# First batch of a two-stage kernel: row and channel DFT as plain matmuls on TensorE in place of VectorE folds, with the sine tables ahead of the first exponential

## The chip, the cores and the metric

The kernel runs on one core of a Trainium2 chip. The metric is the device time of one execution in microseconds (us); lower is better. All times below are of that one core. The engines are called as in the profile: PE (TensorE, matmuls), DVE (VectorE), ACT (ScalarE), POOL (GpSimd), SP (the queue that issues most transfers).

## What is computed

There are 8 batches of 8 heads, with 576 rows and 64 values to a head. First comes an attention with feature maps, then a Fourier mixing of the whole 576 x 512 block of a batch, a normalisation and a two-layer network (FFN):

```python
proj = einsum('bhsd,df->bhsf', x, w_phi); proj -= max(abs(proj), -1)
phi = concatenate([exp(proj), exp(-proj)])
num = einsum('bhsf,bhfd->bhsd', phi(q), einsum('bhsf,bhsd->bhfd', phi(k), v))
x = num / (einsum('bhsf,bhf->bhs', phi(q), sum(phi(k))) + 1e-6)   # (8, 576, 512) over heads
u = x + real(fft(fft(x, axis=1), axis=2))
un = (u - mean(u)) / sqrt(var(u) + 1e-6)
out = u + relu(un @ w_ch1) @ w_ch2                                # 512 -> 2048 -> 512
```

## The kernel before

The work of a batch b is split into streams, Python generators that issue a few instructions for each step: keys, queries and values are fetched (K, Q, V), turned (A, B; for batch 0 on PE: G, J), projected and exponentiated (P, T, R, S), combined and mixed (M, with D for the folds), normalised (N, U) and sent through the FFN (F). One-off streams are C (arguments of the sines), H (the sine tables), Z (constant pads), W (the FFN's weights) and Y (fill matmuls of ones, result unused, in `stir`). A string `PLAN` of one letter a step says in which order the steps are issued; each engine runs its instructions in that order, and waits where an operand isn't there. So the order of an engine's queue is fixed by PLAN, and the times are not.

The FFN of batch 0 can begin when its input `UT` is there; until then PE has only the attention of batches 0 and 1, the mixing of batch 0 and the fill. From then on the FFN of one batch runs beside the attention and mixing of the next.

The mixing of a batch is a real DFT over 576 rows and then over 512 channels. The 576 rows of X lie in 5 chunks of 128 partitions (the last half full). `folded` uses the symmetry of sines and cosines: DVE adds and subtracts mirrored rows and mirrored channels of X into R (lines 869 to 893), subtracts a term of row 0 that a matmul with ones has spread over the partitions (pm, lines 994, 998 and 1048) and folds once more into CEO (line 1007, 1053). PE then needs only 3 chunks: `along_rows` multiplies with the tables CS and SS (cosine and sine over rows, psD and px, lines 1019 to 1058), ACT and DVE copy psD to DT and ET, and the channel DFT multiplies with CD and SD (pu, line 1087). DVE adds pu to X (line 1072 for batch 0), UN is X less its mean, four transposes on PE turn it (put, line 1142) and DVE or ACT copies it to UT (lines 1146, 1148). The first FFN matmul (psf, line 1207) needs chunks 0 and 2 of UT.

For batch 0, the tables SS, CS, SD, CD are made by four ACT sines (lines 212 to 223), behind the last exponential of batch 0. ACT has to load a function table when it changes between exponentials and sines. The arguments are made by DVE and POOL (`constants`, lines 175 to 204). At the start, ACT loads the exponentials' table and runs `warm`.

In PSUM, `pb` has three buffers for psD, pu, put, psq and psf, `pj` two for psk and psh, and `pk` one. A matmul waits until the buffer that it takes has been read. KT is batch 1's turned keys (transfers of line 387 on SP, from KS, which POOL's line 258 fetches); psk is their projection (line 468), MK its largest absolute values (line 488).

Of the kernel before, what the change touches and what calls it, by code (L numbers as in the profile page):

```python
# [9 lines left out]
AT = mybir.ActivationFunctionType  # L10
# [13 lines left out]
    "CYCCZYCYGGTRTTGZZGTYZWRTJTSRJGRJYSTPTSPKTTPJMJRTSSKMYMBMPTQPTPQVTMZTMQTMMTPCMMMTTMTHDYAMMYHHDHHKYYVD"  # L24
    "YDTMTMHTKZMRMSRTYMTTMNYMRVTYQNNMTNTSMNMBFFFRFFNUFNFSMFWFUNRUFQUMTPSFFMNTFPSMTFTNUPYFQMUFPPTVMFTPMTPF"
    "FMMFTTFMFAUTFMMFFMFMFMFMFFKRFPDFFTTTFFDVFFDRFTFFVDFFKTSRFQVFFFFMFFMTFRFFFFFSMTMFFMRTFFMSTMFTFNNMFMQF"
    "PTMMFTFSFMPTFFPTTPMFFFFMFSNBFMFPTQMFFAFMNPFTFMNMFFMFFMMFTTFFURMFFVFRMFFSTFFMFFMFVFTTPFFFFRFPDFFFTPFF"
    "FFFVDDRFFFQFDTMTFFQTSMKFFFMFFFKMRMFTTTMMFNNFFMMFMQFMFFSSMTFMTFFFNFSTPPMFTFMBFPTFPAMFFFMFNTFKMMFFFNFM"
    "FMFFMFFUMQMFFVMFFFTTPFFFFMTFFRFTTFFVFFFRFFRFDFFFFDFDFFDPTFMFTTFFFFMKFRFTMSFMRFFMFTSPMFNTMPQNSFFFFQMM"
    "MMTTTFFBMSFFFFTPMTFSFFMFFMTPVMFFFFMTPNFFNNMMMFFMAFFFMUFMFKMFFFMFFTTDTTFRFFSFFFFRVFFTMFFFFFRPTFFDFFFD"  # L30
    "RFFFTDFMFVKTPFFFFFMTMBQMFFRSFMFTSTSTMMKFFFNNSFMMFMMFTFMFPTMKFFFFPTPMTFFMFFFNMFTPPMFFFTNFQMNMVFFMFQMF"
    "MFFMUFFMFFVMAFFFFTTTTFDRFRFFTFSFFFFMRFFQFFFDFFTFFFDFFRFVDFTFMFFTTMFFMFFMFRSMFQTTTMFTQFNFMSVFFMFFTNPM"
    "MFMSTPMTFFFFSMTPPMFTFFMPPFBAFMFPFMFNNFMMVFMFMFFFMTTFRMNUFFFFFMRFFFMFFFSTFFMFFPTFFTFFFDDFFFRFTFFFDFDV"
    "RFFFMFTTFFMFMTMFRFFSMFFSFMTTNTFFMFNMMFFFMMFTFMPSTFNFFFPTFMFFTMPFFFFMPSPMFFTMFFPFTMNFFFNMFMFFFUMFMFMF"
    "FFFMFFMFMFFFFFDFFDFFFFFDFFFDFMFFFMFMFFMMFFMFNFMNFFFFFFMFFFFFMNFFFMFFNFFFFFFFFFFFFFFFNUFFFFFFFFFFFFFF"
    "FFFFFFFFFFFFFFFFFFFFFFFFFFFFFFFFFFFFF"
# [4 lines left out]
def kernel(  # L41
# [81 lines left out]
    nc.vector.memset(mhalf[:], -0.5)  # L123
    keep = const.tile([128, 1], F32, name="keep")
# [18 lines left out]
    def count_first():  # L143
# [12 lines left out]
        nc.vector.tensor_single_scalar(out=ident[:], in_=tn, scalar=0.0, op=ALU.is_equal)  # L156
# [3 lines left out]
    def count_rest():  # L160
        count(pick_i[:], [[1, 32]], 0, -1)
        nc.vector.tensor_single_scalar(
            out=pick_i[:], in_=pick_i[:], scalar=31, op=ALU.bitwise_and
        )
        nc.vector.tensor_scalar(
            out=pick[:], in0=pick_i[:], scalar1=0.0, scalar2=-2.0, op0=ALU.is_equal, op1=ALU.mult
        )
        nc.vector.tensor_copy(out=ident_b[:], in_=ident[:])
# [3 lines left out]
    turns, turns_c = gs[:, 1024:1024 + 3 * NK], gc[:, C:2 * C]  # L172

    def constants(b):
        nc.vector.tensor_scalar_mul(out=pn[:, 0:3], in0=pc[:, 0:3], scalar1=1.0 / S)
        nc.vector.tensor_scalar_mul(out=pn[:, 3:4], in0=pc[:, 3:4], scalar1=1.0 / C)
        for j in range(3):
# [3 lines left out]
            nc.gpsimd.tensor_scalar(  # L181
                out=turns[:, NK * j:NK * j + NK], in0=rs, scalar1=pn[:, j:j + 1], scalar2=MAGIC,
                op0=ALU.mult, op1=ALU.add,
            )
        yield
# [23 lines left out]
    def sines(b):  # L209
# [20 lines left out]
        yield  # L230

# [8 lines left out]
    def pads(b):  # L240
        for X_ in (QPHP, QPHN):
            nc.gpsimd.memset(X_[:, :, 576:640], 1.0)
            yield
        for X_ in (V4P, V4N):
# [54 lines left out]
    def load_first():  # L299
# [17 lines left out]
        nc.scalar.activation(out=warm[:], in_=halfpi[:], func=AT.Exp)  # L317
# [580 lines left out]

    def first_heads():
        X = xpool.tile([128, 5, C + 1], F32, tag="X", name="X")  # L900
        R = fpool.tile([128, 3, 2, 512], F32, tag="R", name="R")
        CEO = fpool.tile([128, 3, 2, 2, 128], BF16, tag="CEO", name="CEO")
        HI = HIS[0]
        folds[0] = folded(X, R, HI)

# [31 lines left out]
        return X, R, CEO, HI  # L937

    def heads(b):
        if b == 0:  # L940
            return (yield from first_heads())
# [49 lines left out]
    def mixing(b):  # L991
        X, R, CEO, HI = yield from heads(b)
# [21 lines left out]
        def along_rows(i, mat, dst):  # L1014
            if b == 0:
                for mt in range(2):
                    ps = pb.tile([128, 512], F32, tag="pb", name="psD")
                    for c in range(3):
                        nc.tensor.matmul(
                            ps[:, 0:NF], lhsT=CEO[0:deep[c], c, abs(mt - i), i, :],  # L1020
# [370 lines left out]
```

## Time and profile before

| | |
|---|---|
| median of 3 runs | 414.81 us (414.77 to 420.89) |
| profiled execution, its own time | 415.15 us |
| its span, first to last instruction | 413.4 us |
| mean granted PE clock | 0.995 |
| busy: PE, DVE, ACT, POOL | 394.6, 319.4, 303.8, 215.1 us |
| PE busy in us 0 to 50 and 50 to 100 | 43.2 and 47.8 us |
| last value of batch 0's X (line 919) ready | 34.9 us |
| first FFN matmul (line 1207) starts | 50.90 us |
| first matmul of the FFN of batch 1 starts | 104.45 us |

The profile covers one execution. A row of the timeline has the start in us, the length in us, the engine, the line, the instruction with the tiles that it writes and reads, and in brackets the idle time ahead of it with what ended that. PE's rows overlap, because matmuls are pipelined: two rows of the same form with different counts give the time of one more matmul. A row of the windows has, for each engine, its busy time in that stretch and the number of instructions, then the granted PE clock.

### The profile page before, as it was taken

Reading aid. Unit: us, or ns where it says so; the run is one execution under the profiler, and the core shown is the slowest. Engines: PE = TensorE matmul, PEld = TensorE weight load, DVE = VectorE, ACT = ScalarE, POOL = GpSimd, SP = SyncE. Lnnn points to the kernel's source line nnn. Section 1 sums busy time; section 2 is a strip of 40 time slices with the busy share of each in tenths; the row PEclk is TensorE's granted clock in tenths of the full one; section 3 lists DMA queues with packets and bytes.
Section 4 is the critical chain, followed back from the end, with each engine's and each line's share of the span. In section 5 each row is a group of like instructions: output and inputs, shape, how many; then the busy total and the mean of one; then the engine's idle time right before and its main releaser. Section 6 shows DMA issues by size and latency. Waiting matters only on the chain.

```text
span 413.4 us, 10526 instructions
## 1 busy us (share of the span) xinstructions
PE 394.6 (95%) x4194; PEld 259.5 (63%) x4194; DVE 319.4 (77%) x662; ACT 303.8 (73%) x617; POOL 215.1 (52%) x279
## 2 busy tenths in 40 slices
PE   7898999989999989999899999999999999999994
PEld 3574577535856568566756577566856586658563
DVE  5979887999699867797689878888799768875101
ACT  6988999658958886688868886789758885544350
POOL 8997695774466753707658373649271343201000
PEclk9999899999999999999999999999999999999999
DMA  7999979898674899654965979757952141106103
GB/s 210 221 170 158 181 100 185 87 118 128 102 118 58 67 179 141 63 92 83 129 97 65 156 104 142 80 72 116 117 97 52 46 83 21 27 14 114 24 23 90
DMA packets 108520, 42.71 MB, mean 103 GB/s; under 512 B 82615, under 2 KB 103479, under 8 KB 108471
## 3 DMA queue, kind: packets, MB, share of 16 engines
q0 software_dynamic: 46272, 16.60, 37.1%
q1 hardware_dynamic: 61703, 24.85, 32.9%
q10 hardware_dynamic: 496, 0.59, 0.6%
q8 instruction: 33, 0.54, 0.5%
q14 instruction: 16, 0.13, 0.1%
HBM read 36.77 MB, written 9.44 MB: 112 GB/s over the span
## 4 chain that ended last, share of the span: by engine, by line
PE 69%; DVE 13%; DMA 8%; ACT 4%; POOL 3%; issue 2%; DVEq 0%; POOLq 0%; SPq 0%; ACTq 0%
PE psf L1207 29%; PE pso L1224 19%; DMA UT<-UN 4%; PE kv L853 3%; PE psD L1035 2%; PE psk L468 2%; DMA KT<-KS 2%; PE pu L1087 2%; DMA KS<-in_k_dram 2%; PE psq L522 2%; PE psh L563 1%; DVE MK L488 1%; PE pso L1250 1%; DVE cb L969 1%; DVE X L1077 1%
## 5 line engine op out<-in xcount | busy, mean ns | idle before, releaser
L1207 PE MATMUL psf<-UT,W1b 128*128 128x320 bf16 (+1 forms) x1024 | 141.1, 286 | 2.9 <-DMA UT<-UN 2.8
L1224 PE MATMUL pso<-W2b,HT 128*128 128x512 bf16 x496 | 120.5, 379 | 0.0
L1207 PEld LDWEIGHTS <-W1b 128*128 128x128 bf16 x1024 | 94.6, 98 | 30.9 <-issue 3.8
L1212 ACT ACTIVATE HT<-psf 128x320 bf16<-128x320 f32 x128 | 53.9, 444 | 25.7 <-PE psf L1207 19.5
L1224 PEld LDWEIGHTS <-HT 128*128 128x128 bf16 x496 | 45.2, 98 | 43.2 <-issue 0.4
L975 POOL TENSOR_TENSOR X<-cb,rd 128x640 f32<-128x640 f32 x28 | 35.1, 1254 | 52.9 <-DVE rd L973 29.6
L443 POOL TENSOR_TENSOR VCn<-VS,VCn 128x512 bf16<-128x512 bf16 x28 | 29.9, 1067 | 43.4 <-ACT VCn L438 36.6
L530 DVE TENSOR_REDUCE MQ<-psq 128x8 f32<-128x1024 f32 (+1 forms) x32 | 34.3, 1088 | 17.8 <-PE psq L522 17.4
L1230 DVE SCALAR_TENSOR_TENSOR X<-pso,rs,X 128x512 f32<-128x512 f32 x31 | 23.0, 743 | 28.2 <-PE pso L1224 28.0
L1214 ACT ACTIVATE HT<-psf 128x512 bf16<-128x512 f32 x64 | 37.3, 602 | 6.8 <-PE psf L1207 6.6
L488 DVE TENSOR_REDUCE MK<-psk 128x8 f32<-128x1024 f32 x28 | 33.8, 1210 | 1.4 <-ACT KPn L474 1.4
L474 ACT ACTIVATE KPp<-psk 128x1024 bf16<-128x1024 f32 x28 | 28.8, 1027 | 7.8 <-PE psk L468 7.5
L258 POOL DMA_DIRECT2D QS<-in_q_dram x49 | 33.4, 688 | 1.1 <-issue 1.1
L1133 ACT ACTIVATE UN<-X,MV 128x512 bf16<-128x512 f32 (+1 forms) x35 | 25.2, 726 | 11.5 <-DVE MV L1158 8.0
L572 ACT ACTIVATE QPHP<-psh 128x1024 bf16<-128x1024 f32 x28 | 28.9, 1031 | 4.8 <-PE psh L563 4.5
L474 ACT ACTIVATE KPn<-psk 128x1024 bf16<-128x1024 f32 x28 | 28.7, 1025 | 1.7 <-DVE MK L488 1.6
L443 POOL TENSOR_TENSOR VCp<-VS,VCp 128x512 bf16<-128x512 bf16 x28 | 29.9, 1067 | 0.0
L572 ACT ACTIVATE QPHN<-psh 128x1024 bf16<-128x1024 f32 x28 | 29.0, 1036 | 0.0
L1157 DVE BATCH_NORM_STATS2 st<-X 128x6 f32<-128x512 f32 (+1 forms) x40 | 27.1, 678 | 0.2
L1077 DVE TENSOR_TENSOR X<-pu,X 128x512 f32<-128x512 f32 (+3 forms) x49 | 23.5, 526 | 4.6 <-PE pu L1087 4.5
L955 PEld LDWEIGHTS <-QPHP 128*128 128x128 bf16 x280 | 20.5, 99 | 7.8 <-DVE cb L969 3.8
L1173 POOL TENSOR_TENSOR rs<-VE,mhalf 128x5 f32<-128x5 f32 (+1 forms) x9 | 10.3, 1148 | 24.8 <-DVE VE L1172 24.7
(462 smaller groups left out, 797.2 us busy)
## 6 DMA issues: line engine op xcount, KB each, us to landing
out_dram<-X SPq DMA_DIRECT2D x31, 128.0 KB
out_dram<-X SPq DMA_DIRECT2D x15, 256.0 KB
KS<-in_k_dram POOLq DMA_DIRECT2D x7, 512.0 KB, 8.2
VS<-in_v_dram POOLq DMA_DIRECT2D x14, 256.0 KB, 4.8
W1b<-in_moe_w_ch_dram POOLq DMA_DIRECT2D x1, 2048.0 KB, 15.3
W2b<-in_moe_w_ch_dram POOLq DMA_DIRECT2D x1, 2048.0 KB, 16.1
QS<-in_q_dram POOLq DMA_DIRECT2D x28, 64.0 KB, 3.6
QS<-in_q_dram POOLq DMA_DIRECT2D x7, 256.0 KB, 5.6
```

Of the source, the lines that this page charges most:

```text
L258: nc.gpsimd.dma_start(out=pieces[i][0], in_=pieces[i][1])
L443: nc.gpsimd.tensor_tensor(out=VC[:, hs, :, 0:D], in0=values[b][0][:, hs, :].rearrange("p h (j d) -> p h j d", d=D), in1=VC[:, hs, :, D:D + ...
L474: nc.scalar.activation(out=KP[:, hs, :, :].rearrange("p e (jp jj) f -> p jj (e jp) f", jj=2), in_=psk[:], func=AT.Exp, scale=sgn,)
L488: nc.vector.tensor_reduce(out=MK[:, 2 * pr:2 * pr + 2, :].rearrange("p e (jp jj) -> p jj (e jp)", jj=2), in_=tiles[pr][:], axis=AX.X, op=A ...
L530: nc.vector.tensor_reduce(out=o, in_=i[:], axis=AX.X, op=ALU.max, apply_absolute_value=True)
L572: nc.scalar.activation(out=o, in_=psh[:], func=AT.Exp, scale=sgn)
L975: nc.gpsimd.tensor_tensor(out=X[:, :, at:at + 2 * D].rearrange("p c (e d) -> p e c d", e=2), in0=cb[:, :, :, 0:D], in1=rd[:].to_broadcast( ...
L1077: nc.vector.tensor_tensor(out=to, in0=more, in1=to, op=ALU.add)
L1207: nc.tensor.matmul(ps, lhsT=W1b[:, cc, 128 * hh:128 * hh + 128], rhs=UT[:, cc, lo:hi], start=(cc == 0), stop=(cc == NCC - 1),)
L1212: nc.scalar.activation(out=HT[:, hh, lo:hi], in_=ps, func=AT.Relu, scale=-1.0)
L1214: nc.scalar.activation(out=HT[:, hh - 1:hh + 1, lo:hi], in_=psw[:].rearrange("p (a n) -> p a n", a=2), func=AT.Relu, scale=-1.0,)
L1224: nc.tensor.matmul(po[:], lhsT=HT[:, hh, at:at + 128], rhs=W2b[:, hh, :], start=(hh == 0), stop=(hh == NHH - 1),)
```

## The change

Batch 0 gets no folds. `less_first` only subtracts the spread row 0 from X and writes bf16 (XB); it works first on the outer quarters of channels (heads 0, 1, 6, 7), then on the inner ones. `first_rows` multiplies all 5 chunks of rows with the tables, 4 quarters by cosine and sine, 8 groups of 5 matmuls of 320 columns in place of 15 of 289, and copies each group (4 on DVE, 4 on ACT) to EO. `first_channels` sums 16 matmuls of 256 columns to one pu, three times, in place of 4. It needs further tables (`full`, and SN = -SS) that POOL and DVE derive from the four of the sines. XB, EO and the rest lie in R's and the tables' old space. Batches 1 to 7 keep the folds; their code only moves to `folded_rows`.

The sines come ahead of the first exponential: the first table that ACT loads is that of the sines, and it loads that of the exponentials once. DVE instead of POOL makes the first product of the sines' arguments (`turns`), and `ident`, `pick` behind it. `stir` has 7 steps instead of 15. PLAN is new in its first 500 letters or so, which are batches 0 and 1; the rest is the same.

```diff
-        nc.vector.tensor_single_scalar(out=ident[:], in_=tn, ...)   # in count_first
...
+        nc.vector.tensor_single_scalar(out=ident[:], in_=tn, ...)   # in count_rest
...
-            nc.gpsimd.tensor_scalar(
+            nc.vector.tensor_scalar(
                 out=turns[:, NK * j:NK * j + NK], in0=rs, scalar1=pn[:, j:j + 1], scalar2=MAGIC,
...
+        yield
+        count_rest()
...
+        for z, T_ in ((0, CD), (1, SD)):
+            nc.gpsimd.tensor_tensor(
+                out=full[:, z], in0=T_[:].rearrange("p (k m) -> p k m", k=2),
+                in1=flip[:].unsqueeze(1).to_broadcast([128, 2, 256]), op=ALU.mult,
+            )
...
+        nc.vector.tensor_single_scalar(out=SN, in_=SS[:], scalar=-1.0, op=ALU.mult)
...
-        nc.scalar.activation(out=warm[:], in_=halfpi[:], func=AT.Exp)
+        nc.scalar.activation(out=warm[:], in_=halfpi[:], func=AT.Sin)
...
+    def less_first(X, XB, PM):
+        HI = HIS[0][:].rearrange("p i (a n) -> p (i a) n", n=128)
...
+        for outer in (True, False):
+            qs = slice(0, 4, 3) if outer else slice(1, 3)
+            nc.scalar.copy(out=HI[0:1, qs], in_=XQ[0:1, 4, qs])
+            pm = pb.tile([128, 2, 128], F32, tag="pb", name="pm")
+            nc.tensor.matmul(pm[:], lhsT=ones_b[:], rhs=HI[:, qs], start=True, stop=True)
+            if outer:
+                nc.scalar.copy(out=PM, in_=pm[:])
+            yield
+            for cs in (slice(0, 2), slice(2, 4)):
+                late = outer and cs.start
+                (nc.gpsimd if late else nc.vector).tensor_tensor(
+                    out=XBQ[:, cs, qs], in0=XQ[:, cs, qs],
+                    in1=(PM if late else pm[:])..., op=ALU.subtract,
+                )
...
+    def first_rows(XB, EO):
+        for quarter in (0, 3, 1, 2):
+            for i in range(2):
+                ps = pb.tile([128, 512], F32, tag="pb", name="psD")
+                for c in range(5):
+                    deep = 65 if c == 4 else 128
+                    mat = (SS if c in (2, 3) else SN) if i else CS
+                    nc.tensor.matmul(
+                        ps[:, 0:NK], lhsT=XB[0:deep, c, 128 * quarter:128 * quarter + 128],
+                        rhs=mat[0:deep, 2 if c == 4 else c % 2, :], start=(c == 0), stop=(c == 4),
+                    )
+                if i:
+                    nc.scalar.copy(out=EO[:, i, quarter, :], in_=ps[:, 0:NK])
+                else:
+                    nc.vector.tensor_copy(out=EO[:, i, quarter, :], in_=ps[:, 0:NK])
+                yield
+
+    def first_channels(t, pu, EO):
...
+        todo = [(quarter, i, n) for quarter in (0, 3, 1, 2) for i in range(2) for n in range(2)]
+        for z, (quarter, i, n) in enumerate(todo):
+            nc.tensor.matmul(
+                pu[0:M, n, :], lhsT=EO[:, i, quarter, 128 * t:128 * t + M],
+                rhs=tables[quarter][n][i], start=(z == 0), stop=(z == len(todo) - 1),
+            )
...
-        for i in range(15):
+        for i in range(7):
```

ACT's queue at its start, before: KT and K4p, K4n, KPp, KPn belong to the keys of batch 0, the last four are exponentials.

```order
L317 ACT_TABLE_LOAD
L317 ACTIVATE warm<-halfpi 128x1
L178 ACTIVATE ga<-ga,pc 128x320 x3
L195 ACTIVATE ga<-gc,pc 128x512
L357 CAST wphi_95<-wphi_f 128x128
L350 CAST KT_169<-pst 128x256
L350 CAST KT<-pst 128x512
L761 ACTIVATE K4p<-ps_229 128x512
L762 ACTIVATE K4n<-ps_229 128x512
L776 ACTIVATE KPp<-psk 128x2x4x128
```

The same place of ACT's queue in the change:

```order
L340 ACTIVATE warm<-halfpi 128x1
L181 ACTIVATE ga<-ga,pc 128x320 x3
L217 ACTIVATE SS<-gs 128x960
L200 ACTIVATE ga<-gc,pc 128x512
L221 ACTIVATE CS<-ga,halfpi 128x960
L380 CAST wphi_95<-wphi_f 128x128
L373 CAST KT_169<-pst 128x256
L373 CAST KT<-pst 128x512
L226 ACTIVATE SD<-ga 128x512
L228 ACTIVATE CD<-ga,halfpi 128x512
L784 ACT_TABLE_LOAD
L784 ACTIVATE K4p<-ps_231 128x512
```

The four sines and the table load now stand ahead of K4p; the two later table loads are gone, and the 44 instructions from K4p to the last exponential of batch 0's queries are the same ones.

DVE's queue behind the last combination of batch 0 (the reciprocal and X of heads 2 and 3), before: R and CEO are the folds.

```order
L917 RECIPROCAL rd_815<-pn__794 128x10
L919 TENSOR_TENSOR X<-pn__794,rd_815 128x2x5x64
L869 TENSOR_TENSOR R<-X 128x2x256 x2
L875 TENSOR_TENSOR R<-X 128x255
L878 TENSOR_TENSOR R<-X 128x1
```

The same place in the change, up to the first copy of psD; R is here the space in which XB and EO lie, ga that of SN.

```order
L967 RECIPROCAL rd_784<-pn__763 128x10
L969 TENSOR_TENSOR X<-pn__763,rd_784 128x2x5x64
L936 TENSOR_TENSOR R<-X,pm 128x2x2x128
L941 SCALAR_TENSOR_TENSOR R<-X,keep,pm 65x2x128
L250 TENSOR_SCALAR ga<-SS 128x960
L936 TENSOR_TENSOR R<-X,pm 128x2x256 x2
L941 SCALAR_TENSOR_TENSOR R<-X,keep,pm 65x256
L1111 CAST R<-psD 128x320
```

Six instructions stand where there were 18 up to CEO's last, and the outer quarters' subtraction stands behind the last combination, though those heads are ready earlier.

119 lines of the change are left out of this document (71 added, 48 removed).

## The prediction

> **What bounds the kernel now.** I first read the page's busy shares and the chain of work that ended last.
>
> ```profile
> PE 394.6 (95%) x4194; PEld 259.5 (63%) x4194; DVE 319.4 (77%) x662; ACT 303.8 (73%) x617; POOL 215.1 (52%) x279
> ...
> PE 69%; DVE 13%; DMA 8%; ACT 4%; POOL 3%; issue 2%; DVEq 0%; POOLq 0%; SPq 0%; ACTq 0%
> ```
>
> PE carries the end. Its busy time holds fill, so what counts is when useful matmuls become dense: when the FFN of batch 0 starts. PE's timeline:
>
> ```profile
> 50.90 2.34 PE L1207 MATMUL psf<-UT,W1b 128*128 128x256 bf16 x20
> 53.08 0.39 PE L1142 MATMUL put<-ident_b,UN 128*128 128x128 bf16 x4
> 53.30 1.04 PE L1207 MATMUL psf<-UT,W1b 128*128 128x256 bf16 x8
> ```
>
> It starts at 50.90. The reader also takes a price from here: 12 more matmuls of 256 columns cost 2.34 - 1.04 = 1.30 us, 0.108 each, so 0.135 for 320 columns. Next I asked for windows of the time before that start, and behind it.
>
> ```profile
> 8.07:31.93 23.86, 21.18 (x320) 14.69 (x321) 21.34 (x41) 22.30 (x46) 22.66 (x28) 1.00 1.04 206
> ```
>
> From batch 0's first exponential to its last, ACT (fourth number) works 22.30 of 23.86 us: **this stretch is bound by ACT**, and what starts it late ends it late.
>
> ```profile
> 51.00:70.00 19.00, 19.00 (x260) 14.12 (x259) 15.75 (x36) 18.97 (x42) 14.04 (x17) 1.00 0.96 143
> 70.00:77.80 7.80, 7.64 (x108) 5.42 (x107) 6.78 (x19) 5.36 (x14) 5.26 (x5) 1.00 1.32 107
> 77.80:95.00 17.20, 15.30 (x102) 7.21 (x100) 17.13 (x29) 10.08 (x19) 13.72 (x19) 1.00 0.90 108
> ```
>
> Behind the FFN's start ACT (18.97 of 19.00) and PE are full, later DVE is (17.13 of 17.20, the fold of batch 1) with PE idle for 1.9 us. So a later FFN start is passed on to the end but for those 1.9 us; PLAN is the same behind it.
>
> **The first exponential.** The table arguments of the sines come from POOL and DVE:
>
> ```profile
> 4.33 1.56 POOL L181 TENSOR_SCALAR gs<-ga,pn 128x320 f32<-128x320 f32 x3 [0.82 <-DVE pn L176]
> ```
> ```profile
> 5.92 0.94 DVE L186 TENSOR_SCALAR gs<-gs 128x960 f32<-128x960 f32 x1 [1.73 <-POOL gs L181]
> 6.98 1.44 DVE L189 TENSOR_TENSOR gs<-gs,ga 128x960 f32<-128x960 f32 x1
> ```
>
> They are ready at 6.98 + 1.44 = 8.42. In the change DVE makes POOL's three products itself (about 1.1 us by L186's 0.94 for as many elements) and does not stand 1.73 us waiting, but has pick and ident between: I take 7.4 (7.0 to 7.9). ACT before:
>
> ```profile
> 4.71 0.71 ACT L195 ACTIVATE ga<-gc,pc 128x512 f32<-128x512 f32 x1
> 5.41 0.30 ACT L357 CAST wphi<-wphi_f 128x128 bf16<-128x128 f32 x1
> 7.01 0.37 ACT L350 CAST KT<-pst 128x256 bf16<-128x256 f32 x1 [1.30 <-PE pst L345]
> 7.59 0.58 ACT L350 CAST KT<-pst 128x512 bf16<-128x512 f32 x1 [0.21 <-PE pst L345]
> 8.07 0.60 ACT L761 ACTIVATE K4p<-ps 128x512 bf16<-128x512 f32 x1
> ```
> ```profile
> 31.52 0.39 ACT L690 ACTIVATE QPHN<-ph 128x256 bf16<-128x256 f32 x1
> 31.93 1.28 ACT L212 ACT_TABLE_LOAD   x1
> 33.23 1.00 ACT L212 ACTIVATE SS<-gs 128x960 bf16<-128x960 f32 x1
> 34.14 1.08 ACT L216 ACTIVATE CS<-ga,halfpi 128x960 bf16<-128x960 f32 x1
> 35.12 0.61 ACT L221 ACTIVATE SD<-ga 128x512 bf16<-128x512 f32 x1
> 35.64 0.71 ACT L223 ACTIVATE CD<-ga,halfpi 128x512 bf16<-128x512 f32 x1
> ```
>
> By the new order ACT runs from 7.4: SS 1.00, tc2 0.71, CS 1.08, the casts 0.30 + 0.37 + 0.58, SD 0.61, CD 0.71, table load 1.28. That is 6.64, less some 0.1 for each overlap (33.23 to 34.14 is 0.91 for a row of 1.00): 6.0. The first exponential starts at 13.4 (13.0 to 14.3) in place of 8.07, **5.3 us later**. The sines were hidden before, since ACT had nothing urgent at 31.9 to 37; here they stand ahead of the bound engine. The Trainium skill's page "ScalarE: Activation LUTs", section "What ACT_TABLE_LOAD costs", puts a switch at 1.28 us of load and 1.38 us of drain. The row above shows 1.28, and SS starts 1.30 behind the load's start, so no such drain is seen here; with it the first exponential would be at 14.8.
>
> The 44 instructions that follow are the same ones, 22.3 us. They waited for 1.56 us before. Some of those waits (for keys, tables of DVE) go, since data lie ready; others come, because the products of POOL with VC start later by as much and PE is colder. Between 0 and 1.6 I take 0.9: the last exponential ends at 36.6 against 31.91, 4.7 later.
>
> **X and the DFT of rows.** On DVE:
>
> ```profile
> 34.10 0.82 DVE L919 TENSOR_TENSOR X<-pn__794,rd 128x640 f32<-128x640 f32 x1
> 34.96 1.30 DVE L869 TENSOR_TENSOR R<-X 128x512 f32<-128x512 f32 x2
> ```
> ```profile
> 42.76 0.17 DVE L1053 CAST CEO<-R 128x6 bf16<-128x6 f32 x1
> 42.84 1.22 DVE L488 TENSOR_REDUCE MK<-psk 128x8 f32<-128x1024 f32 x1
> 44.55 0.46 DVE L1029 CAST DT<-psD 128x289 bf16<-128x289 f32 x1 [0.49 <-PE psD L1019]
> ```
>
> X was complete at 34.92, so at 39.5 now (its two outer folds no longer delay it, 0.1). The folds ran from 34.96 to 42.93, 8 us with one MK reduction. In place stand three subtractions of 0.65 (half of L869's 1.30), two of 65 partitions and 256 columns at about 0.4, and SN. SN (960 bf16) isn't in the trace: between 0.42 (UT's copy of 512 bf16, below) and 0.94 (L186); I take 0.55, nearer the copy, which is bf16 too. Sum 3.3: XB is complete at 42.8, **so DVE gives back 4.7**. POOL's share of the subtraction and the further tables lie beside this; its queue has them at about 36 to 44, ahead of pu.
>
> PE waited here for batch 1's keys:
>
> ```profile
> 40.07 0.40 PE L468 MATMUL psk<-wphi,KT 64*128 64x128 bf16 x8 [1.76 <-DMA KT<-KS]
> 40.40 1.63 PE L1019 MATMUL psD<-SS,CEO 128*128 128x289 bf16 x6
> ```
>
> The same psk stands ahead of the first psD in the change. KS is issued about 0.4 later on POOL (four products of VC fewer are ahead of it, all some 4.7 later), so it is there at 40 to 41.
>
> ```profile
> 26.34 0.93 POOL L258 DMA_DIRECT2D KS<-in_k_dram  x1
> ```
>
> PE then has 8 groups x 5 x 0.135 = 5.4 us. The first two run at 40.7 to 42.1, the third needs the buffer of pm that DVE reads until 42.8. From there each odd group waits for its copy on ACT (0.46 by the row of DT) behind batch 1's exponentials of 1.0 us (KPp, KPn, KPp, KPn and V4 stand between the four copies in ACT's queue). ACT's queue, walked through: K4p and K4n to 41.6, KPp and KPn to 43.4, copy 43.9, KPp 44.8, copy 45.3, KPn 46.2, copy 46.7, V4 47.6, last copy 48.1. Then pu, 16 x 0.108 + 0.17 = 1.9, ends at 50.0. Before:
>
> ```profile
> 46.55 0.69 DVE L1072 SCALAR_TENSOR_TENSOR X<-pu,X 128x512 f32<-128x512 f32 x1 [0.98 <-PE pu L1087]
> ```
>
> So pu is **3.5 us later** (46.5 to 50.0): of the 4.7 of the folds PE's longer DFT leaves 1.1.
>
> **From pu to the FFN.** Before, 4.4 us. DVE's rows:
>
> ```profile
> 49.41 0.49 DVE L1122 TENSOR_SCALAR UN<-X,nm 128x512 bf16<-128x512 f32 x1
> 49.82 0.68 DVE L1072 SCALAR_TENSOR_TENSOR X<-pu,X 128x512 f32<-128x512 f32 x1
> 50.43 0.08 DVE L1072 DVE_READ_ACCUMULATOR X<-pu,X 128x1 f32 x1
> 50.43 0.42 DVE L1146 COPY UT<-put 128x512 bf16<-128x512 bf16 x1
> ```
>
> In the change the second pu (16 matmuls, at 51.9) is added (0.68) ahead of UN of chunk 2, MK (1.22) stands between UN and the copy to UT, and the third pu (1.8) and batch 1's psh (0.4) stand ahead of psf on PE. UN ends at 53.2, put at 53.6, pu at 55.3, psh at 55.7: psf starts at 55.7, **4.8 later**. What now lies ahead of psf no longer lies behind it: psh 0.4, a psq of 8 matmuls 0.3, and the one fill that PE had behind it:
>
> ```profile
> 60.66 1.04 PE L1322 MATMUL idle<-ones_b 128*128 128x512 bf16 x4
> ```
>
> Together 1.7. ACT, full there, has one exponential (1.06) fewer behind psf, and so agrees with +3.1 to +3.7. In the stage of DVE's fold, one reduction of 1.2 us now stands behind the fold; I take 0.7 off for that, of the 1.9 that PE idles. The sum is 4.8 - 1.7 - 0.7 = **+2.4 us** on the profiled execution's 415.15, which lies 0.34 above the median: 417.2 on the median's scale.
>
> **The rivals.**
> *No change, because the delay is absorbed later (414.8).* If the 44 instructions run without a wait (-0.9), the tables are ready at 7.0 (-0.4) and the new order fills all of PE's 1.9 us (-1.2 more than taken), the sum is -0.1. PE's idle time at 77.8 to 95 speaks for it, ACT's full 19 us ahead of that against it. It decides at 2.4 us of saved waits.
>
> *Not slower, because PE's row DFT keeps up with XB (415.1).* The place is the four copies on ACT. If they don't hold the buffers, four groups are done when XB is complete at 42.8, four more take 2.7, a copy 0.5, and pu ends at 47.9, not 50.0: +2.4 - 2.1 = +0.3. The 8 us of folds that go speak for it; the exponentials between the copies, four of 1.0 us and V4, speak against it. From a last copy at 46 on it holds. Both cases together give 412.7, and only so is the kernel clearly faster.
>
> *Slower, because PE loses its clock (419.7).* Six later psD, and the window in which the first six ran (granted clock last but two):
>
> ```profile
> 43.97 0.91 PE L1019 MATMUL psD<-CS,CEO 128*128 128x289 bf16 x6
> ```
> ```profile
> 41.00:42.00 1.00, 1.00 (x7) 0.35 (x7) 0.96 (x3) 1.00 (x2) 0.12 (x1) 0.50 1.42 206
> ```
>
> At clock 0.50 six took 0.72 more. The drop followed a wait of 1.76 with little work around it. In the change the fill at the start is 4 matmuls, not 12, PE waits some 4 us for KT's casts on ACT, and the DFT is three times as long. Three us of it at half clock cost 1.5, colder chains among the exponentials 1.0: 2.4 + 2.5 = 4.9. For it speaks the missing fill, against it the 8 fill matmuls that still stand ahead of psk. The Trainium skill's page "TensorE: Matmul & The Clock Gate", section "Part 1: The HAM clock gate", has the clock at half after a window of about 3.4 us without work, and full again after as long of work. The half clock here came after less idle time than that, so the trace is less lenient; by the rule the DFT would stay at full clock and the sum be 417.2.
>
> That the change doesn't do what it says I leave out: the order has one load of the exponentials' table and no fold in batch 0.
>
> **How the numbers follow.** Forecast 0.47 (416 to 419), no change 0.15, not slower 0.15, both 0.07, loss of clock 0.16. Range: the early table and no waits together with PE's idle time reach 414.8, with the DFT unheld 412.7; waits of 1.6 and tables at 7.9 add 1.2, the clock 2.5, so 421. I give 412.5 to 421.5. Some 2% (8.3 us) is about what a measurement tells from no change; below 406.5 no case reaches, so faster by over 2% has 0.01, slower (above 423.1, clock lost in both stages and keys late) 0.04, within 2% 0.95.
>
> **What the profile after would show.** Right: first exponential at 13 to 14, last near 36.6, X at 39.5, last psD copy near 48, psf near 55.7 with PE's timeline otherwise alike, and the FFN of batch 1 some 2.4 later than 104.45. Wrong: SS starting before 7, or a stretch of exponentials under 22 us; psD groups back to back with pu before 48; a clock of 0.50 in the windows of the DFT; or an FFN of batch 0 shorter by more than 2.4 from psf to psf.

## The result, and the profile after

The change makes the kernel **slower**: a median of 431.56 us (430.89 to 433.01, 4 runs) beside 416.40 for the kernel before in the same comparison, a ratio of 1.0351 with a 95% interval of 1.0258 to 1.0444 (the ratio is that of the means, so it is not quite the quotient of the medians). 417.2 had been predicted, with a range of 412.5 to 421.5. The profiled execution took 433.01 us; its span is 431.2, against 413.4 before: 17.8 us, all of it from the first 70 us.

| us in the profiled execution | before | predicted | after |
|---|---|---|---|
| first exponential starts | 8.07 | 13.4 | 15.29 |
| last exponential of batch 0 ends | 31.9 | 36.6 | 47.65 |
| X of batch 0 complete | 34.92 | 39.5 | 50.46 |
| folds done / XB complete | 42.9 | 42.8 | 56.47 |
| last copy of psD | | 48.1 | 62.18 |
| first UN starts (on ACT) | 47.66 | | 65.09 |
| first psf starts | 50.90 | 55.7 | 69.97 |
| span | 413.4 | 415.8 | 431.2 |

The busy shares and the chain that ended last, of after:

```profile
PE 396.4 (92%) x4196; PEld 266.8 (62%) x4224; DVE 323.0 (75%) x651; ACT 302.5 (70%) x615; POOL 219.9 (51%) x284
PE 70%; DVE 12%; ACT 6%; POOL 6%; issue 3%; DMA 2%; DVEq 0%; POOLq 0%; ACTq 0%
```

They hardly differ from before: POOL is busy for 4.8 us more, DVE for 3.6, PE for 1.8 and ACT for 1.3 less, and PE carries 70% of the chain as it did (69%). So most of the 17.8 us must be waits. A window of after from the first exponential of batch 0 to its last shows where (ACT is the fourth engine), and one inside its second half what the clock (last number but two) does:

```profile
15.29:47.65 32.36, 23.66 (x305) 16.30 (x305) 23.89 (x34) 22.47 (x45) 19.59 (x26) 0.84 0.92 145
36.00:44.00 8.00, 8.00 (x96) 5.28 (x93) 3.35 (x9) 4.90 (x10) 3.79 (x5) 0.50 1.11 123
```

ACT works 22.47 us, as before (22.30), but in 32.36 us, not 23.86. **ACT no longer bounds the stretch; it waits 9.9 us in it.** Its timeline in after, with the start of the sines, the table load, the first exponential and the waits:

```profile
9.06 1.00 ACT L217 ACTIVATE SS<-gs 128x960 bf16<-128x960 f32 x1 [4.26 <-DVE gs L194]
14.00 1.28 ACT L784 ACT_TABLE_LOAD   x1
15.29 0.60 ACT L784 ACTIVATE K4p<-ps 128x512 bf16<-128x512 f32 x1
...
37.70 1.09 ACT L662 ACTIVATE QPHN<-psn 128x512 bf16<-128x512 f32 x2 [7.54 <-PE psn L686]
...
47.27 0.38 ACT L713 ACTIVATE QPHN<-ph 128x256 bf16<-128x256 f32 x1
50.55 0.40 ACT L928 CAST HI<-X 1x256 bf16<-1x256 f32 x1 [2.90 <-DVE X L969]
...
61.75 0.43 ACT L1109 CAST R<-psD 128x320 bf16<-128x320 f32 x1
...
65.09 0.72 ACT L1201 ACTIVATE UN<-X,nm 128x512 bf16<-128x512 f32 x1 [1.07 <-DVE nm L1192]
```

One wait is 7.54 us. QPHN is an exponential of batch 0's queries; psn, its input, subtracts row maxima, which `turn_m` (lines 716 to 730, the same code as before) splits on DVE into three bf16 parts by four tiny instructions of 20 columns and turns on PE (pt). It runs twice, for the outer heads and for the inner. What released psn is one step further back, on PE and DVE of after:

```profile
35.39 0.34 PE L724 MATMUL pt<-ident_b,m 128*96 128x128 bf16 x1 [6.01 <-DVE m L722]
...
51.17 3.48 PE L1396 MATMUL idle<-ones_b 128*128 128x512 bf16 x8
...
55.38 0.85 PE L1104 MATMUL psD<-CS,R 128*128 128x320 bf16 x5
...
69.97 1.05 PE L1281 MATMUL psf<-UT,W1b 128*128 128x256 bf16 x8
```
```profile
2.96 3.24 DVE L184 TENSOR_SCALAR gs<-ga,pn 128x320 f32<-128x320 f32 x3
...
28.02 4.09 DVE L719 CAST m<-MQ 128x20 bf16<-128x20 f32 x1
32.14 0.98 DVE L720 TENSOR_TENSOR ml<-MQ,m 128x20 f32<-128x20 f32 x1
33.15 1.08 DVE L721 CAST m<-ml 128x20 bf16<-128x20 f32 x1
34.26 1.07 DVE L722 TENSOR_TENSOR m<-ml,m 128x20 bf16<-128x20 f32 x1
...
41.08 0.18 DVE L719 CAST m<-MQ 128x20 bf16<-128x20 f32 x1
```

The first CAST, of 20 columns, takes 4.09 us, and all four 7.3; the inner `turn_m`, at 41.08, runs at 0.18 for each. What differs is POOL. Its timeline in after, beside `turns` (L184) and beside the outer `turn_m`:

```profile
3.44 0.61 POOL L263 MEMSET QPHP<- 128x512 bf16 x1
...
27.31 1.64 POOL L281 DMA_DIRECT2D KS<-in_k_dram  x2
28.97 1.08 POOL L858 TENSOR_TENSOR VCn<-HT,VCn 128x512 bf16<-128x512 f32 x1
...
32.02 1.05 POOL L858 TENSOR_TENSOR VCp<-HT,VCp 128x512 bf16<-128x512 f32 x1
33.02 2.36 POOL L281 DMA_DIRECT2D QS<-in_q_dram  x4
```

From 27.31 to 35.38 POOL has no gap: issues, four products of values (VCn, VCp), issues. The CAST starts under the first issues and ends with the third product (32.1), the next instruction ends with the fourth product (33.1), the last with the issues (35.3). Before, `turn_m` had rows like these:

```profile
20.69 0.34 DVE L696 CAST m<-MQ 128x20 bf16<-128x20 f32 x1
...
25.65 0.77 DVE L696 CAST m<-MQ 128x20 bf16<-128x20 f32 x1
```

The longer one ends at 26.42, and so does a product of POOL beside it (26.38): a little of this was there before. The rows say which theory to test: **POOL holds DVE, so PE and ACT stand, and PE's clock falls** (8.00 of 8.00 us busy at 0.50 in the window above, behind 6 us of idling). The rivals are the new DFT itself, the new place of the sines by itself, and the clock as a cause rather than an effect. As a yardstick the experiments use the start of the first UN, since in nearly every kernel below the span is that start plus 365.7 to 366.7 us (365.7 before, 366.1 after; 367.2 in e10 and 371.4 in e4). These starts and spans are those of the profiled executions. Before's first UN:

```profile
47.66 0.72 ACT L1127 ACTIVATE UN<-X,nm 128x512 bf16<-128x512 f32 x1
```

### The profile page after: what moved, and what is told of

It is laid out like the page before. It is cut to its first block, busy times and chain, and to the rows that moved or that the text cites. A ratio compares the mean times of both kernels' runs of the same rounds, so it can differ in the third digit from the quotient of the medians.

```text
span 431.2 us, 10551 instructions
## 1 busy us (share of the span) xinstructions
PE 396.4 (92%) x4196; PEld 266.8 (62%) x4224; DVE 323.0 (75%) x651; ACT 302.5 (70%) x615; POOL 219.9 (51%) x284
## 4 chain that ended last, share of the span: by engine, by line
PE 70%; DVE 12%; ACT 6%; POOL 6%; issue 3%; DMA 2%; DVEq 0%; POOLq 0%; ACTq 0%
PE psf L1281 27%; PE pso L1298 18%; PE kv L876 4%; PE pso L1324 3%; POOL X L1023 3%; PE psD L1065 3%; DMA UT<-UN 2%; DVE cb L1017 2%; PE pu L1161 2%; PE psh L586 2%; DVE tg L1010 2%; PE psq L545 1%; PE psk L491 1%; PE pu L1125 1%; DVE R L892 1%
## 5 line engine op out<-in xcount | busy, mean ns | idle before, releaser
L1281 PE MATMUL psf<-UT,W1b 128*128 128x320 bf16 (+1 forms) x1024 | 139.7, 286 | 1.6 <-DMA UT<-UN 1.6
L1298 PE MATMUL pso<-W2b,HT 128*128 128x512 bf16 x468 | 117.4, 379 | 1.7 <-issue 0.5
L1286 ACT ACTIVATE HT<-psf 128x320 bf16<-128x320 f32 x128 | 53.0, 439 | 24.5 <-PE psf L1281 18.7
L892 DVE TENSOR_TENSOR R<-X 128x512 f32<-128x512 f32 x28 | 18.6, 716 | 8.9 <-POOL X L1023 8.9
```

The costliest lines, as they stand in the source:

```text
L1281: nc.tensor.matmul(ps, lhsT=W1b[:, cc, 128 * hh:128 * hh + 128], rhs=UT[:, cc, lo:hi], start=(cc == 0), stop=(cc == NCC - 1),)
L1286: nc.scalar.activation(out=HT[:, hh, lo:hi], in_=ps, func=AT.Relu, scale=-1.0)
L1298: nc.tensor.matmul(po[:], lhsT=HT[:, hh, at:at + 128], rhs=W2b[:, hh, :], start=(hh == 0), stop=(hh == NHH - 1),)
```

## The experiments

### POOL held DVE: the order, the clock, and the wait by itself

**e1** moves four kinds of steps of POOL (S products, K and Q issues, H tables) behind the outer `turn_m` in PLAN.

```diff
-...MRTKMKSPTJJMSQTHMPPTTPMQ...
+...MRTKMPTJJMTMPSKSQHPTTPMQ...
```

> The changed kernel with POOL's work of 27.3 to 35.4 us (the scaled values of the last two pairs, the big keys' and the first queries' DMA issues) put behind the outer turn_m; VectorE's program is the same. Theory A (turn_m's four small VectorE instructions are held while POOL runs without a gap, and TensorE and ACT starve behind them): the four take 1.0 to 1.6 us together instead of 7.3, the exponentials of psn start by 31.5 instead of 37.70, the granted clock does not fall to 0.50 between 34 and 43, the last exponential of the batch ends at 37.5 to 40 instead of 47.65, and the kernel takes 420 to 425 us instead of 431.6. Theory B (the clock falls because fill was taken out, whatever VectorE does): the clock still reads 0.50 to 0.6 between 34 and 43 and the kernel stays at 428 to 432. Theory C (the sines ahead of the exponentials carry the loss alone): 430 to 432, since they stay where they are.

**Measured:** 429.81 us, ratio 1.0356 [1.0296, 1.0417]; first UN at 60.88 (4.2 earlier) and span 426.8 in the profiled execution. DVE of e1:

```profile
28.17 0.18 DVE L719 CAST m<-MQ 128x20 bf16<-128x20 f32 x1
...
33.34 2.22 DVE L719 CAST m<-MQ 128x20 bf16<-128x20 f32 x1
```

The outer `turn_m` is free, and now the inner one lies under the products, which moved (VCn at 33.44, VCp at 34.45): 2.22, 1.08, 1.09 and 1.18 us for its four instructions. The trace bears the theory out, but the time missed the 420 to 425 us that the theory had been given, and the ratio doesn't separate e1 from the change: a meeting was moved, not removed.

**e2** leaves the order and takes the clock's fall away: 28 fill matmuls stand ahead of the outer pt.

```diff
+            if outer:
+                for _ in range(7):
+                    fill = pk.tile([128, 512], F32, tag="pk", name="idle")
+                    for x in range(4):
+                        nc.tensor.matmul(fill[:], lhsT=ones_b[:], rhs=ones_b[:]..., start=True, stop=True)
```

> The changed kernel with 28 fill matmuls (128x512) on TensorE ahead of the matmul that waits for the outer turn_m; POOL and VectorE as in the changed kernel. Theory A: turn_m still takes about 7.3 us and the exponentials of psn start near 37; only what TensorE lost at half clock between 35.4 and 48 comes back, 2 to 4 us: 427.5 to 430. Theory B (the clock is the cause): 10 us or more come back, 417 to 422. Theory C: 431.

**Measured:** 431.19 us, 1.0383 [1.0340, 1.0425]; first UN 63.21. PE of e2 and its window (the clock is the last but two):

```profile
29.19 7.51 PE L727 MATMUL idle<-ones_b 128*128 128x512 bf16 x28
36.75 0.22 PE L733 MATMUL pt<-ident_b,m 128*96 128x128 bf16 x1
```
```profile
36.00:44.00 8.00, 7.94 (x134) 5.29 (x132) 4.55 (x12) 5.68 (x12) 3.74 (x5) 1.00 0.99 123
```

The clock stays at 1.00, though the fill itself ended 1.4 us too late for pt (36.75, not 35.39). UN gains 1.9 and the time nothing that can be measured. **The lost clock is real (1.9 us of UN here; by estimate 3.3, if the 1.4 of the fill's lateness passed through in full), and a consequence:** with the clock held, the other 15.5 of the 17.4 us stay. The Trainium skill's page "TensorE: Matmul & The Clock Gate", section "Part 1: The HAM clock gate", has the full clock back after about 3.4 us of sustained work; the trace of after doesn't agree, since small matmuls kept PE busy for 8.00 us at 0.50.

**e11** measures the wait by itself: it leaves the whole computation out. DVE runs a CAST and a TENSOR_TENSOR of 20 columns in turn, beside nothing, beside products of POOL, fills, DMA issues and iotas, and with an operand in PSUM.

```diff
+        nc.gpsimd.tensor_tensor(out=big[0][:], in0=src[:], in1=mul[:], op=ALU.mult)   # 8 in a row; or memset, or DMA issues
+        nc.vector.tensor_copy(out=cst[0][:], in_=src[:, 0:20])
+        nc.vector.tensor_tensor(out=sub_[0][:], in0=src[:, 0:20], in1=one_[:], op=ALU.subtract)   # 4 of each
```

> Leaves the whole computation out and measures the disputed cost by itself: VectorE runs small instructions (copies and subtractions of 128x20) while POOL runs in turn nothing, products of 128x512, fills of 128x512, DMA issues, and counts (iota); then the same products against VectorE instructions that read PSUM, and against a 128x320 scaling. Theory A (whatever POOL runs holds VectorE's instructions that read SBUF alone): 0.18 us each beside nothing, 0.8 to 1.1 us beside products, held as well beside fills, DMA issues and counts, and about 0.2 us for those that read PSUM. Rival A1 (only POOL's products with two inputs from SBUF hold): no hold beside fills, counts and DMA issues. Rival A2 (turn_m's wait was for data, not for POOL): 0.18 us everywhere.

**Measured** (54.81 us for all of it): DVE of e11 beside nothing, beside products, beside 14 fills, beside issues, and from PSUM beside products; then POOL's product and last fill.

```profile
3.74 0.18 DVE L73 CAST cst<-src 128x20 bf16<-128x20 f32 x1
...
4.91 1.22 DVE L93 CAST cst<-src 128x20 bf16<-128x20 f32 x1
6.05 0.17 DVE L94 TENSOR_TENSOR sub<-src,one__65 128x20 f32<-128x20 f32 x1
...
15.26 6.44 DVE L119 CAST cst<-src 128x20 bf16<-128x20 f32 x1
...
22.58 0.34 DVE L142 CAST cst<-src 128x20 bf16<-128x20 f32 x1
...
31.50 0.17 DVE L178 CAST cst<-ps 128x20 bf16<-128x20 f32 x1
```
```profile
4.84 1.26 POOL L84 TENSOR_TENSOR big<-src,mul 128x512 bf16<-128x512 f32 x1
...
21.15 0.52 POOL L117 MEMSET big<- 128x512 bf16 x1
```

A CAST from SBUF waits for the running product of POOL (1.22 beside 1.26, so 0.18 becomes 1.22); from PSUM it doesn't (0.17). Beside fills it waits for the whole train of 14 (until 21.67), and beside iotas of 0.55 us each the CASTs took 0.28 to 0.62. The Trainium skill's page "SBUF — State Buffer", section "Who interferes with whom", describes this: VectorE and GpSimd share a port pair under an exclusive lock, casts and copies can take it in modes that use two ports, the one that came second is blocked for the whole instruction, and a DVE instruction with at most one input from SBUF and in none of these modes is free. The product and PSUM rows agree; the train of fills goes beyond it, since the CAST was let in between none of the 14 instructions, and so do the products and issues in after (4.09 us for one CAST). A TENSOR_TENSOR took 0.17 here, where it began at 6.05, just ahead of the next product (6.06), and 0.98 in after, beside a running product. Two things stay open: why a CAST gets in between products of POOL here and not in after, and why two instructions under issues took 1.08 and 1.07 us in after (at 33.15 and 34.26), while here, where all eight lay beside the first issue, none took over 0.34.

**e6** frees both: in an order like e1's, with the products in two parts, a tiny copy on POOL reads the last result of the inner `turn_m`, so that the products behind it can't start earlier.

```diff
+            if not outer:
+                nc.gpsimd.tensor_copy(out=gate[:], in_=m3[0:1, 2, 0:1])
...
-...MRTKMPTJJMTMPSKSQHPTTPMQTMTMTMPMTTMM...
+...MRTKMPTJJMTMPSPTTPMTMPSTMTMKQQHMTTMM...
```

> The changed kernel with POOL's work kept off both turn_m's: the third pair's values behind the outer one, the last pair's values and the DMA issues behind a small POOL instruction that waits for the inner one. Theory A (POOL's train holds VectorE's small instructions wherever the two meet): both groups of four take 0.7 to 1.0 us, ACT waits under 1 us for psn at both places, X is complete at 41.5 to 43.5 instead of 50.46 (47.69 with only the outer one free), the first UN starts at 55 to 57 instead of 65.09, and the kernel takes 422 to 425 us. Rival (it was TensorE's clock): the clock stays at 0.5 somewhere between 30 and 42, first UN 59 or later, 426 to 430. What is then left above the kernel before, some 8 us, is the sines' place.

**Measured:** 427.91 us, 1.0307 [1.0272, 1.0343]; first UN 58.73, span 424.9. All eight instructions of the two `turn_m` take 0.18; the first of each in e6:

```profile
28.17 0.18 DVE L720 CAST m<-MQ 128x20 bf16<-128x20 f32 x1
...
33.34 0.18 DVE L720 CAST m<-MQ 128x20 bf16<-128x20 f32 x1
```

The 32.36 us of exponentials are 27.3 (15.46 to 42.74), and ACT waits 4.6 us in them, not 9.9. So 6.4 us of UN, in the profiled executions, were the holding of DVE behind the first exponential, with the clock that followed. That is less than expected (UN at 55 to 57, 422 to 425 us). Some of it comes back as waits for the products that now run later: kv on PE waits 1.70 us for one, and kvh on ACT 1.14 at 37.00. Behind that wait the clock fell here too, to 0.51 from 38 to 41, so the sign that the rival (the clock as the cause) had been given is there as well, and the time lies in its range (426 to 430); against it speak e2 and the order of events, first the wait, then the clock.

### The parts of the change alone

**e4** is the kernel before with only the sines early: the old folds, the old order, the four sines ahead of the first exponential.

```diff
-    "CYCCZYCYGGTRTTGZZGTYZWRTJ...
+    "CYCCZYHCYHGGHCHTRTTGZZGTYZWRTJ...
...
-        nc.scalar.activation(out=warm[:], in_=halfpi[:], func=AT.Exp)
+        nc.scalar.activation(out=warm[:], in_=halfpi[:], func=AT.Sin)
```

> The kernel before (VectorE's folds, its order) with only the four sines put ahead of the first exponential. Theory C's share by itself: the first exponential starts at 13 to 14 instead of 8.07; behind the last exponential one table load and four sines (1.3 + 3.3 us) fall out, which then hide nothing: X complete 4.5 to 6 later than 34.92 and the kernel at 418 to 421.5 if turn_m is not held, which is 25 to 45 per cent of the change's 15 us. If the sines' place carried the whole loss: 428 to 432. If the two table loads and sines that fall out behind pay for it: 414 to 417.

**Measured:** 426.03 us, 1.0273 [1.0214, 1.0332]; first UN 55.96. ACT and PE of e4:

```profile
15.32 0.60 ACT L761 ACTIVATE K4p<-ps 128x512 bf16<-128x512 f32 x1
```
```profile
163.83 1.86 PE L1207 MATMUL psf<-UT,W1b 128*128 128x256 bf16 x8 [4.74 <-DMA UT<-UN]
```

The first exponential is 7.25 us later, X 8.5 (4.5 to 6 had been expected), UN 8.3. **The place of the sines alone, in this order, makes the old kernel slower by 2.7%.** In the profiled execution, the longest of four (429.14 us), it also waits 4.74 us for a transfer at 163.83 (its span is UN plus 371.4, not 365.7); why the transfer came so late stays open.

**e3** is the other part: the change's DFT, with the sines behind the last exponential as before, before's order at the start, `turns` on POOL, SN ahead of the further tables and 15 steps of fill.

```diff
-        nc.scalar.activation(out=warm[:], in_=halfpi[:], func=AT.Sin)
+        nc.scalar.activation(out=warm[:], in_=halfpi[:], func=AT.Exp)
...
-            nc.vector.tensor_scalar(
+            nc.gpsimd.tensor_scalar(
...
-        for i in range(7):
+        for i in range(15):
```

> The new DFT over all rows and channels with the sine tables behind the last exponential and the order of the two batches taken from the kernel before (turns on POOL as there). Theory A: the first exponential starts near 8.1 and the outer turn_m takes about 1.2 us, as before; X is complete near 35; the sines of the rows end near 35.5, XB is complete by 39 to 40.5, the eight groups of the row DFT end by 44 to 46, and the kernel takes 412 to 418 us. If the new DFT itself carries a good part of the loss: 422 or more, with the row DFT or the channel DFT ending over 5 us later than 46.5.

**Measured:** 422.51 us, 1.0196 [1.0130, 1.0262], so that the new DFT seemed to carry a good part of the loss. X is complete at 34.58, as before, but UN starts at 52.91, 5.3 later. PE of e3:

```profile
37.31 4.69 PE L1393 MATMUL idle<-ones_b 128*128 128x512 bf16 x12
...
42.40 0.86 PE L1101 MATMUL psD<-CS,R 128*128 128x320 bf16 x5
```

Twelve fill matmuls stood ahead of the first psD for 4.69 us, far longer than the wait that they were to cover. **e5** puts the fill ahead of XB, SN right behind SS and nothing between the two DFTs (its SN lay over the arguments of SD, so that its channel sines have other values; the instructions and their sizes are the same).

```diff
+        nc.vector.tensor_single_scalar(out=SN, in_=SS[:], scalar=-1.0, op=ALU.mult)   # behind SS, not behind CD
...
-        for i in range(15):
+        for i in range(12):
```

> The new DFT with the sines behind the last exponential (as the run with the sines late), but the fill matmuls that stood between XB and the row DFT put ahead of XB, the negated sines made as soon as the first sines are there, and no fill between the row DFT and the channel DFT. From the first UN to the end the kernels so far took 365.7 to 366.5 us, so the time follows the first UN. Theory A' (the new DFT by itself costs next to nothing, what the run before lost there was fill in its way): the row DFT starts by 39.5 instead of 42.40, the first UN starts at 47.5 to 49.5 instead of 52.91, and the kernel takes 415 to 418 us. Rival (the row DFT and channel DFT on TensorE are the bound whatever stands ahead of them): first UN 51.5 or later, 420 to 423 us.

**Measured:** 418.28 us, 1.0072 [1.0048, 1.0097]; first UN 49.61. Before the first pu, PE waits at psk, a projection of batch 1's keys that isn't needed yet, in e5:

```profile
46.40 0.40 PE L488 MATMUL psk<-wphi,KT 64*128 64x128 bf16 x8 [1.45 <-DVE MK L508]
```

**e9** puts that psk behind the first pu, takes the fill between pm and psD out and lays SN elsewhere.

```diff
-    SN = ga[:, 1024:1504]...
+    SN = gs[:, 1024:1504]...
...
-        for i in range(12):
+        for i in range(10):
```

> The new DFT with the sines behind the last exponential, trimmed further: no fill between XB and the row DFT, the last keys of the next batch behind the first part of the channel DFT, the negated sines in a place of their own. If the new DFT costs about what the folds cost (theory A'): the row DFT starts at 37.2 to 38 (38.11 before this trim), the first UN at 46.2 to 47.8 (before 47.66), and the kernel takes 412.5 to 416.5 us, level with the kernel before or just under it. Rival (the sixteen matmuls for each third of the channel DFT and the eight groups of the row DFT bound it): first UN at 48.5 or later, 417 us or more.

**Measured:** 415.49 us (12 runs) beside 415.38, ratio 0.9992 [0.9966, 1.0018]; first UN 47.30. PE of e9, the first psD 5.2 us ahead of e3's:

```profile
37.25 0.84 PE L1101 MATMUL psD<-CS,R 128*128 128x320 bf16 x5
```

**The new DFT costs nothing and gives nothing**: 8 us of folds go from DVE, and PE's 40 row and 48 channel matmuls with their copies fill the time. X to UN takes 12.7 us both before (34.92 to 47.66) and here (34.58 to 47.30).

### The early sines, with the meetings taken out

**e7** is e6 with the arguments of the sines ahead of `count_rest` (pick, ident) and the pads of POOL behind them.

```diff
-    "CCCZZCYHZCHWGGHZCHT...
+    "CCCCCYHZZHCWGGHZZHT...
```

> The kernel of the run with both turn_m's free, and POOL's pads, VectorE's small constants behind the arguments of the sines instead of ahead of them. Theory A: turns takes 1.0 to 1.6 us instead of 3.24, the first sine starts at 5.8 to 7 instead of 9.06, the first exponential at 12 to 13.3 instead of 15.29, the first UN 2 to 3 us earlier than in the run with both turn_m's free, 419.5 to 422.5 us. Rival (the casts of the keys or the channel sines' arguments on POOL bound the start): first exponential at 14.5 or later, no gain.

**Measured:** 432.95 us, 1.0410 [1.0372, 1.0449], a miss: `turns` takes 1.54, not 3.24, and SS starts at 6.83, not 9.22, yet UN starts at 65.61, 6.9 later than in e6. DVE and POOL of e7:

```profile
2.96 1.54 DVE L185 TENSOR_SCALAR gs<-ga,pn 128x320 f32<-128x320 f32 x3
...
6.83 2.53 DVE L195 TENSOR_SCALAR ga<-gs 128x960 int32<-128x960 int32 x1
```
```profile
23.71 0.62 POOL L844 TENSOR_TENSOR V4N<-HT,V4N 64x256 bf16<-64x256 f32 x1 [1.71 <-ACT QT L374]
```

Three things took the gain. The moved pads hold the next instructions of DVE (2.53; 0.66 in after), and the first exponential is at 16.50, not 15.46. And the first products of values (V4N) end 2.7 us later, with the load of the first FFN weights (W, 2 MB) issued at 8.80 instead of 12.20. Behind these waits PE's clock was 0.50 from 39 to 48.

**e8** is e6 without the eight fill matmuls ahead of the inner pm, which took 3.48 us in after.

```diff
-...MMTMMMVDDQYHBYDHVV
+...MMTMMMVDDQHBDHVV
```

> The kernel of the run with both turn_m's free, without the eight fill matmuls that stand ahead of the inner pm on TensorE (3.48 us at half clock in the changed kernel). If the fill is in the way: the inner pm follows its HI at once, XB is complete 1.5 to 2.5 us earlier, the first UN 1 to 2 us earlier. If the clock is worth more than the time it takes: the row DFT runs its first groups at 1.3 us instead of 0.68, and the first UN comes 1 to 3 us later. Whole kernel 421 to 427 us.

**Measured:** 428.66 us, 1.0328 [1.0297, 1.0359]; not distinguishable from e6, and UN is 1.4 later: without it PE's clock falls, in a window of e8:

```profile
50.00:54.00 4.00, 4.00 (x27) 2.23 (x26) 2.41 (x6) 3.15 (x4) 3.97 (x5) 0.65 0.55 63
```

In e6 the same window has 1.00. In UN the fill pays for itself there.

**e10** takes all of it together: the arguments first, the pads gated behind the last argument (a tiny copy that reads it), products between the two `turn_m`, issues and tables gated behind the inner one, 9 steps of fill.

```diff
+        nc.gpsimd.tensor_copy(out=gate2[:], in_=tc3[0:1, 0:1])   # ahead of the pads
...
-    "CCCZZCYHZCHWGGHZCHT...MTMPSPTTPMTMPSTMTMKQQHM...
+    "CCCCCYHHCGHHGWZZZZT...MTMPSSPTTPMTMTYMTMYPKQQHM...
```

> The new DFT with the sines ahead of the exponentials as in the change, and every meeting of POOL's trains with VectorE's small instructions that the runs showed taken out: pads behind the sines' arguments (by a small POOL instruction that waits for them), the values of the last two pairs between the two turn_m's, the DMA issues behind the inner one, and eight more fill matmuls. Theory A (what is left is ACT's sines and table load ahead of the exponentials): first sine at 6.5 to 7, first exponential at 12.3 to 13.5, first UN at 52.5 to 55, 420 to 423.5 us: 5 to 8 above the kernel before, and no order of the rest takes that away. Rival (the hold only moves on, as it did in the three runs before): first UN at 57 or later, 425 us or more.

**Measured:** 429.56 us, 1.0339 [1.0302, 1.0376], a miss again, although the first exponential is at 13.24. POOL of e10:

```profile
7.86 0.98 POOL L91 DMA_DIRECT2D W1b<-in_moe_w_ch_dram  x1
...
22.33 0.61 POOL L846 TENSOR_TENSOR V4N<-HT,V4N 64x256 bf16<-64x256 f32 x1 [8.21 <-DMA HT<-in_v_dram]
```

The gate left POOL free, and W was the next in its queue: 2 MB issued at 7.86, and the values of batch 0 (HT), which come by another queue, were waited for until 22.33. **e12** differs from e10 by one letter: W behind the pads.

```diff
-    "CCCCCYHHCGHHGWZZZZT...
+    "CCCCCYHHCGHHGZZZZWT...
```

> The kernel of the run before with the sines ahead and every meeting taken out, except that POOL issues the 2 MB load of the first weights at 12 us again, as the changed kernel does, and not at 7.86, where it went ahead of the last loads of the values (POOL waited for those until 22.33 and 24.20, and TensorE until 28.41). Theory A (what is then left is the sines' place): V4N's product starts by 19, TensorE's wait of 5.95 us for VCp falls to under 1, first UN at 54 to 56.5, 421.5 to 424.5 us, 6 to 9 above the kernel before. Rival (with the sines ahead something else takes up whatever is freed): first UN at 58 or later, 426 us or more.

**Measured:** 422.34 us, 1.0131 [1.0066, 1.0197]; first UN 54.43, 7.8 earlier than in e10. POOL, DVE and the window of the exponentials of e12:

```profile
17.91 1.31 POOL L846 TENSOR_TENSOR V4N<-HT,V4N 64x256 bf16<-64x256 f32 x2 [3.16 <-ACT V4N L842]
```
```profile
31.18 0.98 DVE L723 TENSOR_TENSOR ml<-MQ,m 128x20 f32<-128x20 f32 x1
```
```profile
13.01:38.43 25.42, 23.74 (x321) 16.23 (x321) 18.07 (x34) 22.56 (x45) 19.05 (x29) 1.00 0.79 153
```

This is the change with nearly all its collisions taken out: clock 1.00, 25.42 us for the exponentials, and still 0.7 to 2.0% slower than before. One is left: a TENSOR_TENSOR of the inner `turn_m` takes 0.98 beside POOL's last products of values. **With the sines early no version reached the kernel before; with them late (e9) it is level.** None beats it.

## Why the prediction was wrong, step by step

The 17.4 us of UN split as 7.2 until the first exponential, 8.5 in the exponentials, -0.2 from there to X, and 1.9 from X to UN. By the experiments, freeing `turn_m` took back 6.4 of them (e6) and the further steps to e12 together 4.3; of the 6.8 that are left in e12, 4.9 are its later first exponential. The prediction's own steps, with e12 as the kernel nearest to the one that it described:

| step | predicted | after | e12 |
|---|---|---|---|
| `turns` on DVE | 1.1 | 3.24 | 1.53 |
| SS starts | 7.4 | 9.06 | 6.83 |
| SS to the first exponential | 6.0 | 6.23 | 6.18 |
| ACT's 44 instructions, busy | 22.3 | 22.47 | 22.56 |
| their waits | 0.9 (0 to 1.6) | 9.9 | 2.9 |
| last exponential's end to X | 2.9 | 2.8 | 2.8 |
| X to XB | 3.3 | 6.0 | 4.6 |
| XB to the last psD copy | 5.3 | 5.7 | 5.7 |
| psf later than before | 4.8 | 19.1 | 8.4 |
| given back behind psf | 2.4 | 1.3 | 1.5 |

- **The step that failed is the waits of the 44 instructions: "Between 0 and 1.6 I take 0.9".** The bound was the sum of what ACT had waited in that stretch before. It counted instructions on ACT, and POOL's products only as operands that come later; it didn't ask what POOL, an engine off the chain, would be doing while DVE ran four tiny instructions in the new order. 9.0 of the 15.4 us by which the sum was short are this term. e1, e6 and e11 show its mechanism and e2 that the clock is its follower; e6 took 5.3 of the 9.0 away, and what the rest would be without the clock's fall wasn't separated. The trace of before held a sign: the CAST of 0.77 that ended with a product of POOL.
- **The sines' arguments**: `turns` was priced at 1.1 and took 3.24, with iotas, pads and a product of POOL beside it, and SS started 1.7 late, behind the stated range (7.0 to 7.9). e7, e10 and e12, with the pads later, have 1.53 to 1.54 and SS at 6.83, a little ahead of it: the same failing, a row's duration taken without its neighbour. The table load was priced right: 1.28, with the exponential 1.29 behind its start.
- **What was right**: sines ahead of the bound engine start everything later, 4.9 us in e12 where 5.3 was said, and the folds' 8 us don't pay for it. e4 and e9 show both halves apart; the 1.1 us that the forecast left of the folds' gain aren't there (from X to UN e9 takes as long as before, e12 0.5 more).
- **X to XB** was 2.7 us too short (1.3 in e12, where the clock held): HI (L928) of the outer quarters waits for the last X (2.90 us on ACT), though those heads are ready earlier, and the eight fill matmuls ahead of the second pm ran 3.48 us at half clock. The copies of psD between exponentials on ACT, which decided the rival "PE keeps up", came as forecast (the last ends at 62.18, 5.7 behind XB).
- **The give-back** of 1.7 for work moved ahead of psf is there in part: from psf to the end it takes 1.3 to 1.5 us less, not the 2.4 that the sum had with DVE's fold stage. From UN to the end it takes the same time.
- **The rivals**: none had this mechanism. "No change" needed waits saved, and waits were added. "PE loses its clock" saw the 0.50 that came, at 36 to 44 and 51 to 54, but priced it as a cause, at 2.5 us, and put it into the DFT, whose row matmuls ran at full speed (0.85 for five). The signs listed as showing the forecast wrong had a stretch of exponentials under 22 us, none over it.

Even e12 lies 4.5 us of span above the forecast: its first exponential was 0.4 early, but its waits were 2.0 longer than said, X to XB 1.3, the psD copies 0.4, and 0.9 less was given back. The 9 us from there to the change itself (1.0131 to 1.0351) went when e12 took apart what the change's order lays beside each other: above all products and issues of POOL beside `turn_m`, and pads beside `turns`. It also has two more steps of fill than the change, and what these are worth wasn't separated.

## What to carry to other kernels

Price a small instruction on DVE by what POOL does at the same time: an instruction that costs 0.18 us alone cost 4.09 beside POOL's work, and if a chain over PE and ACT hangs on it, that chain pays. When an order is changed, look for the tiny steps between two engines on the path (casts, splits, turned maxima) and read which neighbours they get, then keep streams of POOL away from them, by the order or a gate. Moving a large load earlier on one queue can delay a small load on another: one letter of the order, W ahead of the pads, made the first UN 7.8 us later.

## What the runs showed of the hardware

- A CAST of 20 columns from SBUF took 0.18 us alone, 1.22 beside products of POOL, 6.44 beside a train of 14 fills that it had to wait out, and 0.17 from PSUM beside products.
- PE's clock stayed at 0.50 for 8 us in which PE was busy 8.00 of 8.00 us with small matmuls; with 28 fill matmuls in the 6 us of idling ahead of them it was 1.00 in the same window.
- A 2 MB load issued at 7.86 in place of 11.84 us let the values of batch 0, on another queue, be used at 22.33 in place of 17.91.
